# Keys of two batches by way of DRAM and a DMA transpose, with a new set-up and transfer model, in a fused block-sparse attention and MLP-mixer kernel

## The chip, the cores and the metric

The kernel runs on one core of one Trainium2 chip. The core has TensorE (PE, matmuls and transposes), VectorE (DVE), ScalarE (ACT), GpSimd (POOL) and SyncE (SP), which compute or issue work each in its own fixed order, and 16 DMA engines. SP, ACT and POOL issue transfers, each from a queue of its own. The metric is the device time of one execution in microseconds (us); lower is better.

## The reference

Four batches, eight heads, 768 positions, head dimension 64. Attention is limited, for each query, to the three blocks of 64 keys with the best gate score and to its own block, and is causal. Then comes one mixer layer: an MLP over positions and an MLP over channels.

```python
k_rep = k.reshape(B, H, n_blocks, block, D).mean(axis=3)
gate_scores = np.einsum('bhsd,bhnd->bhsn', q, k_rep)
gate_scores = np.where(causal, gate_scores, -1000000000.0)
top_idx = np.argsort(gate_scores, axis=-1)[..., -top_k:]
# mask: blocks in top_idx and the own block, and key position <= query position
scores = scale * np.matmul(q, k.transpose(0, 1, 3, 2))
scores = np.where(mask, scores, -1000000000.0)
attn = softmax(scores)
attn_out = np.matmul(attn, v)

x = attn_out.transpose(0, 2, 1, 3).reshape(B, S, H * D)
h = np.maximum(x.transpose(0, 2, 1) @ w_tok1, 0.0) @ w_tok2
u = x + h.transpose(0, 2, 1)
out = u + np.maximum(u @ w_ch1, 0.0) @ w_ch2
```

Inputs and output are fp32. The matmuls of the scores, of attention times V and of the MLPs run in fp16, the gate in fp32, since its order decides which blocks are taken.

## The kernel before, in words

**Pairs.** Two heads of one batch make a pair, numbered i = 0 to 15; pairs 0 to 3 are batch 0, 4 to 7 batch 1, and so on. For each pair:

- `load_qk` (L241) brings keys and queries in as [128, 6, 128] fp32 tiles `kl` and `ql`, in pieces of 256 bytes; `load_v` (L251) does so for the values. SP issues them.
- `transposes` (L330, matmuls on L336) turns each tile by six fp32 transposes on PE against an identity, into the PSUM tiles `tkl` and `tql`. `evac_t` (L339) copies them to SBUF on ACT as `kt` and `qt`; `cast` (L348) makes fp16 of them on POOL, once for each head, into the buffers KA (keys) and Q (queries).
- `ksum` (L354) sums the keys of each block on DVE, `kcopy` (L362) places the sums, `gate` (L372) multiplies queries by them on PE (five fp32 matmuls), and `gm`, `top`, `below`, `bias` (L381 to L413) make from it, on DVE, a bias of 0 or -30000 for each query and block.
- `mask` (L415) transposes the bias on PE, and `put_mask` (L425) writes it into twelve spare rows of Q. The same rows of KA hold an indicator of the block of each key, so that the score matmul adds the bias by itself. KA and Q have 128 rows for each head, 64 of data, twelve of these, and zeros.
- `scores` (L432) on PE, `expo` (L450) on ACT, the causal cut `diag` (L458) on DVE, `av` (L465) on PE, `recip` and `norm` (L477, L485) on DVE.

KA is one tile `KAX` with four slots (R = 4): the pair i uses slot i mod 4.

**MLP.** For each batch: `tok1`, `relu1`, `umix`, `uadd` make u (L497 to L559). u of batch 0 is transposed on PE (`utr`, L561); u of the other batches is stored to a DRAM scratch and loaded back by a transposing DMA (`store_u` L317, `turn_u` L324, issued by SP). Then `ch1` (L579) and `ch2` (L601) on PE with `relu2` and `oadd` on ACT and DVE, and `store` (L617) to the output. The ten weight loads are issued by POOL, which also casts them to fp16 on the way (L637 to L642).

**Who sets the order.** Nothing is decided while the kernel runs. `plan` (L66) is a list scheduler that runs at build time: every piece of work is an `Op` with an engine, an assumed duration, dependences, a priority and the ring buffers that it takes. It yields the order in which the work is emitted, and each engine runs its work in that order. Attention of pair i has priority 10 i and more, its preparation (`pre`) ten less, the MLP of a batch b 1000 (b + 1) and more: MLP work fills what attention leaves. `SP` in the plan are input loads, in the order of priority; `SPO` are stores and turns; both are the same engine. A transfer of assumed length `size` begins 1250 ns after its issue or when the one before has ended, and lands 700 ns after its end. `free` (L69) gives the time from which each engine can take work of the plan.

**The second key route** is in the code already and is taken by pairs i >= VIA; with VIA = 16, by none. In it `load_k8` (L267) loads the keys as [96, 2, 8, 64]: each of 96 rows of SBUF takes eight neighbouring positions, 2 KB in one piece; the tile takes one of the two `kt` buffers. `ksum8` (L277) sums over the eight on DVE, and `ksum_pe` (L284), one fp32 matmul with the constant `blk`, sums groups of eight rows, so that the block sums come without a transposed copy of the keys. `cast_k8` (L291) casts on POOL into the fp16 tile K16, which has 256 columns for each position: 64 keys of the first head, 64 with the block indicator, 64 with the indicator, 64 keys of the second head (`k16_zero` and `k16_ind`, L307 to L315, fill the padding once). `store_k` (L297) writes that to a DRAM scratch, and `turn_k` (L304) brings it back transposed:

```python
return lambda: nc.sync.dma_start_transpose(out=KAX[:, i % R, :, :], in_=T["kscr", i])
```

one transfer that writes the whole slot, keys, indicators and zeros of both heads. SP issues both; the store waits for the cast, the turn for the store and for the scores of pair i - 4.

**Set-up** (L828 to L864) runs before the planned work: constants by ACT's DMA queue, the zero rows of KA and of Q for slots 1 to 3 on POOL, other fills on DVE, and two transfers from ACT's queue that write the indicator rows of KA.

Of the kernel before, what the change touches and what calls it, by code (L numbers as in the profile page):

```python
# [9 lines left out]
FP = mybir.dt.float32  # L10
F16 = mybir.dt.float16
# [17 lines left out]
R = 4  # L29
FIRST = 4  # L30
TRI = 1
EARLY = 1
VIA = 16
UVIA = 1
LEAD = 960.0
WARM, COLD, WARM_END = 120, 20, 17000.0
IDLE = 1e9


class Op:  # L40
# [25 lines left out]
def plan(ops, rings, near=60.0):  # L66


    free = dict(PE=900.0, ACT=5500.0, DVE=4500.0, POOL=5000.0, SP=750.0, SPO=750.0)  # L69
    slots = {name: [(0.0, None)] * n for name, n in rings.items()}  # L70
    dma_free = 0.0
    waiting = {}
    users = {}
    ready = {e: [] for e in free}
    done = {}
    for op in ops:
        n = 0
        for d in op.deps:
            users.setdefault(id(d), []).append(op)
            n += 1  # L80
        waiting[id(op)] = n
        if n == 0:
            ready[op.eng].append(op)

    def finish(op, eng):
        return done[id(op)] + (LAT.get(eng, 33) if op.size == 0 else 60)

    def buf_free(buf, eng):
        t = 0.0
        for u in buf.users:  # L90
            if id(u) not in done:
                return None
            t = max(t, finish(u, eng))
        return t

    order = []
    left = len(ops)
    while left:
        best = None
        for o in [o for o in ready["PE"] if o.prio == IDLE and free["PE"] > WARM_END]:  # L100
            ready["PE"].remove(o)
            done[id(o)] = free["PE"]
            left -= 1
        if not left:
            break
        for e, cand in ready.items():
            if not cand:
                continue
            lst = []
            if e == "SP":  # L110
                if any(x.eng == e and x.prio < min(c.prio for c in cand) for x in ops if id(x) not in done):
                    continue
                cand = [min(cand, key=lambda c: c.prio)]
            for op in cand:
                t = free[e]
                for d in op.deps:
                    t = max(t, finish(d, e))
                ok = True
                for buf in op.takes:
                    first = None  # L120
                    for s, (_, old) in enumerate(slots[buf.ring]):
                        f = 0.0 if old is None else buf_free(old, e)
                        if f is not None and (first is None or f < first[0]):
                            first = (f, s)
                    if first is None:
                        ok = False
                        break
                    t = max(t, first[0])
                    buf.slot = first[1]
                if ok:  # L130
                    lst.append((t, op))
            if not lst:
                continue
            t0 = min(t for t, _ in lst)
            pick = min((x for x in lst if x[0] <= t0 + near), key=lambda x: (x[1].prio, x[0]))
            if best is None or pick[0] < best[0]:
                best = pick
        assert best is not None, "the plan cannot go on"
        t, op = best
        op.start = t  # L140
        for buf in op.takes:
            slots[buf.ring][buf.slot] = (0.0, buf)
        free[op.eng] = t + op.occ
        if op.size:
            begin = max(t + 1250, dma_free)
            dma_free = begin + op.size
            done[id(op)] = dma_free + 700
        else:
            done[id(op)] = t + op.rec
        ready[op.eng].remove(op)  # L150
        order.append(op)
        left -= 1
        for u in users.get(id(op), []):
            waiting[id(u)] -= 1
            if waiting[id(u)] == 0:
                ready[u.eng].append(u)
    return order, max(done.values())
# [3 lines left out]
def kernel(  # L161
# [11 lines left out]
    nc = tc.nc  # L173
# [52 lines left out]
    def op(eng, occ, rec, deps, prio, fn, takes=(), size=0):  # L226
        o = Op(eng, occ, rec, deps, prio, fn, takes, size)
        ops.append(o)
        return o
# [7 lines left out]
    def dve(occ, deps, prio, fn, takes=()):  # L237
        return op("DVE", occ, occ + 84, deps, prio, fn, takes)
# [71 lines left out]
    def k16_ind(y):  # L310
        def f():
            for c in (64, 128):
                nc.gpsimd.tensor_copy(out=K16[y][:, :, c:c + NB],
                                      in_=blk.rearrange("p (o n) -> p o n", o=1).broadcast_to([96, 8, NB]))
        return f  # L315

    def store_u(b):  # L317
# [107 lines left out]
    def put_mask(i, x):  # L425
        def f():
            lo = 64 if x == 0 else 0
            nc.vector.tensor_copy(out=QA[i % R][x][lo:lo + NB, 128:S], in_=T["bps", i][lo:lo + NB, :])  # L428
        return f
# [198 lines left out]
    O = {}  # L628
# [16 lines left out]
    for i in range(NP):  # L645
# [5 lines left out]
        def last_scores(x):  # L651
            return [O.get(("sc", old, x, g)) for g in range(3)]

        if i >= VIA:
            kb = Buf("kt")
            ld = op("SP", 500, 0, [], pre - 12, load_k8(i), [kb], size=1400)
            O["ksum", i] = dve(1100, [ld], pre + 1, ksum8(i))
            nb = Buf("bank")
            O["kpe", i] = pe(115, [O["ksum", i]], pre + 1, ksum_pe(i), [nb])
            O["kcopy", i] = dve(260, [O["kpe", i], O.get(("gate", old))], pre + 1, kcopy(i))  # L660
            nb.users.append(O["kcopy", i])
            y = i % 2
            if i < VIA + 2:
                O["kz", y] = op("POOL", 1100, 1150, [], pre - 1, k16_zero(y))
                O["ki", y] = op("POOL", 400, 450, [O["kz", y]], pre - 1, k16_ind(y))
            O["castk", i] = op("POOL", 1150, 1200, [ld, O["ki", y], O.get(("kst", i - 2))], pre + 3, cast_k8(i))
            kb.users += [O["ksum", i], O["castk", i]]
            O["kst", i] = op("SPO", 600, 0, [O["castk", i], O.get(("cast", "kt", i, 0))], pre + 3.1, store_k(i), size=1600)
            O["kturn", i] = op("SPO", 600, 0, [O["kst", i]] + last_scores(0) + last_scores(1), pre + 3.2, turn_k(i), size=2500)
            O["cast", "kt", i, 0] = O["cast", "kt", i, 1] = O["kturn", i]  # L670
        for t32, src, off in (("kl", k, 0), ("ql", q, 0.1))[i >= VIA:]:
            bf = Buf(t32)
            O[t32, i] = op("SP", 950, 0, [], pre - 12 + off, load_qk(i, t32, src), [bf], size=1900)
# [10 lines left out]
            big.users.append(O[name, i])  # L684
            dst = KA if name == "kt" else QA
            for x in range(2):
                O["cast", name, i, x] = op("POOL", 770, 825, [O[name, i]] + last_scores(x), pre + 4 + off,
                                           cast(dst, name, i, x))
                tb.users.append(O["cast", name, i, x])
            if name == "kt":  # L690
# [20 lines left out]
        mb = Buf("bank")  # L711
        O["mask", i] = pe(280, [O["bias", i]], pre + 4, mask(i), [mb])
        for x in range(2):
            O["put", i, x] = dve(410, [O["mask", i]] + last_scores(x), pre + 4, put_mask(i, x))
            mb.users.append(O["put", i, x])
        for x in range(2):
            for g in range(3):
# [23 lines left out]
            ab.users.append(O["norm", i, x])  # L741

    for n, (at, f) in enumerate(wq):
        after = O["cast", "kt", 3, 1] if n < 2 else O["cast", "qt", 3 + (n - 2) // 2, 1]
        W.append(op("POOL", 700, 0, [after], at, f, size=2900))

    for b in range(B):
        fill = 1000.0 * (b + 1)
# [79 lines left out]
    with tc.manual_schedule():  # L828
# [8 lines left out]
        own1 = np.where(nidx[None, None, :] == mrow, 0.0, MASKV).astype(np.float32)  # L837
        ind_np = (np.arange(S)[None, :] // 64 == nidx[:, None]).astype(np.float16)
        m0_np = (np.arange(128)[None, :] >= np.arange(128)[:, None]).astype(np.float16)
        gbias = const("gbias", np.concatenate([gb1, gb1], axis=2), FP, nc.scalar)  # L840
        own = const("own", np.concatenate([own1, own1], axis=2), FP, nc.scalar)
        ident16 = const("id16", np.eye(128, dtype=np.float16), F16, nc.scalar)
# [7 lines left out]
        nc.vector.memset(QA[0][1][0:64, :], 0.0)  # L850
        for r in range(R):
            nc.vector.memset(bn16[r], 0.0)
        for r in range(1, R):
            nc.gpsimd.memset(QA[r][0][64:128, :].bitcast(FP), 0.0)
            nc.gpsimd.memset(QA[r][1][0:64, :].bitcast(FP), 0.0)
        for r in range(R + 1):
            nc.vector.memset(V16[r][:, :, :, 64:65], 1.0)
        tri = const("tri", (MASKV * (1.0 - m0_np)).astype(np.float16), F16, nc.scalar)
        blk = const("blk", (np.arange(96)[:, None] // 8 == nidx[None, :]).astype(np.float32), FP, nc.scalar)
        m0 = const("m0", np.stack([m0_np, m0_np], axis=1), F16, nc.scalar)  # L860
        ind_dram = nc.inline_tensor(np.ascontiguousarray(np.broadcast_to(ind_np[:, None, :], (NB, R, S))), name="indc").ap()
        for x in range(2):
            lo = 64 * (1 - x)
            nc.scalar.dma_start(out=KAX[lo:lo + NB, :, x, :], in_=ind_dram)  # L864

        for o in order:
            o.fn()
# [33 lines left out]
```

## Time and profile before

| | |
|---|---|
| median of 5 runs | 276.88 us (276.13 to 277.18) |
| the profiled execution, its own time | 276.88 us |
| its span, first to last instruction | 275.1 us |
| granted TensorE clock, mean | 0.998 |
| instructions | 5930 |
| DMA | 34.67 MB, mean 126 GB/s |

The span leaves out 1.8 us of the time, before the first and after the last instruction. Busy time of an engine is the sum over its instructions; of a matmul the modelled end is a little after the start of the next, so the time that one group takes from PE is read from start to start. PEld is the weight load, which overlaps the matmul. A line of the profile names line, engine, operation and tiles as output<-input, with what an idle engine waited for in brackets. The DMA share is the mean over 16 engines; with packets of two queues at once it goes over 1.

### The profile page before, as it was taken

To read this page: it belongs to the slowest core of one execution; us is meant where nothing else is said; L and a number is where in the kernel's file an instruction comes from. 1 tells how busy PE (TensorE), PEld (TensorE's weight loads), DVE (VectorE), ACT (ScalarE), POOL (GpSimd) and SP (SyncE) were. 2 spreads that over 40 slices of the span, in tenths; PEclk is the share of its full clock that TensorE was granted. 3 is DMA by queue.
4 is the path that set the end of the run, shared out by engine and by line. 5 is a ranking of instruction groups with operands and counts; after the bars stand their busy time and mean duration, and the time that the engine had idled before them with its cause. 6 is when DMAs were issued, how large, how long until landed. Compare 5 with 4: busy or idle time off the path is not lost.

```text
span 275.1 us, 5930 instructions
## 1 busy us (share of the span) xinstructions
PE 263.1 (96%) x2309; PEld 174.3 (63%) x2309; DVE 163.5 (59%) x561; ACT 141.9 (52%) x188; POOL 79.1 (29%) x108
## 2 busy tenths in 40 slices
PE   7799989889999999999999999999999999999995
PEld 5678567779777878777777545654455544455543
DVE  5378968799988887886998433325323261243232
ACT  2356988578788888888886602440014410044100
POOL 8467903974543366435440000000000000000000
PEclk9999999999999999999999999999999999999999
DMA  8999999999798599760007222003740006720033
GB/s 168 197 220 203 182 207 224 214 225 218 158 226 167 117 182 200 166 146 2 1 22 194 94 75 80 0 0 116 178 167 2 0 0 209 174 77 0 4 114 114
DMA packets 94628, 34.67 MB, mean 126 GB/s; under 512 B 85672, under 2 KB 91144, under 8 KB 94600
## 3 DMA queue, kind: packets, MB, share of 16 engines
q1 hardware_dynamic: 90272, 29.89, 49.0%
q0 software_dynamic: 3232, 3.93, 8.4%
q10 hardware_dynamic: 1096, 0.47, 0.9%
q8 instruction: 18, 0.29, 0.5%
q14 instruction: 10, 0.08, 0.1%
HBM read 27.21 MB, written 8.65 MB: 130 GB/s over the span
## 4 chain that ended last, share of the span: by engine, by line
PE 72%; DVE 12%; issue 5%; POOL 4%; DMA 2%; ACT 1%; ACTq 1%; SPq 0%; DVEq 0%; POOLq 0%
PE c L606 22%; PE c L585 22%; PE sps L442 8%; PE gps L377 5%; PE aps L473 4%; PE tok L504 3%; PE ups L516 2%; DVE e L462 2%; PE tql L336 2%; DMA ql<-in_q_dram 2%; PE tkl L336 2%; DVE m L394 2%; DVE Q L428 1%; DVE u L524 1%; DVE kst L359 1%
## 5 line engine op out<-in xcount | busy, mean ns | idle before, releaser
L455 ACT ACTIVATE e<-sps 128x1024 f16<-128x1024 f32 (+1 forms) x96 | 84.1, 918 | 19.8 <-PE sps L442 14.3
L585 PE MATMUL c<-uT,wc 128*128 128x256 f16 (+1 forms) x384 | 67.8, 326 | 0.0
L595 ACT ACTIVATE h<-c 128x512 f16<-128x512 f32 x48 | 28.7, 598 | 72.7 <-PE c L585 72.1
L606 PE MATMUL c<-wc,h 128*128 128x512 f16 (+2 forms) x300 | 64.0, 370 | 0.0
L585 PEld LDWEIGHTS <-wc 128*128 128x128 f16 x384 | 37.3, 98 | 23.9
L442 PE MATMUL sps<-Q,KA 128*128 128x512 f16 (+3 forms) x256 | 50.0, 305 | 2.5 <-ACT e L455 1.0
L606 PEld LDWEIGHTS <-h 128*128 128x128 f16 x300 | 28.8, 98 | 32.0 <-issue 0.6
L597 DVE TENSOR_SCALAR h<-c 128x256 f16<-128x256 f32 x48 | 20.2, 420 | 34.9 <-PE c L585 34.9
L614 DVE TENSOR_TENSOR ob<-u,c 128x512 f32<-128x512 f16 (+2 forms) x25 | 16.6, 665 | 39.5 <-PE c L606 39.5
L351 POOL CAST KA<-kt 64x768 f16<-64x768 f32 x32 | 26.8, 838 | 45.3 <-ACT kt L345 44.2
L462 DVE TENSOR_TENSOR e<-e,m 128x256 f16<-128x256 f16 x90 | 32.3, 363 | 12.3 <-ACT e L455 11.3
L442 PEld LDWEIGHTS <-KA 128*128 128x128 f16 x256 | 22.7, 101 | 16.7 <-issue 3.9
L351 POOL CAST Q<-qt 64x768 f16<-64x768 f32 x32 | 26.9, 842 | 4.6 <-ACT qt L345 3.1
L473 PE MATMUL aps<-V,e 128*128 128x65 f16 x672 | 27.1, 193 | 1.2 <-DVE e L462 1.0
L473 PEld LDWEIGHTS <-e 128*128 128x128 f16 x672 | 25.6, 98 | 3.8 <-DVE e L462 1.3
L377 PE MATMUL gps<-ks,qt 128*128 128x24 f32 x160 | 20.3, 269 | 1.9 <-ACT qt L345 1.4
L377 PEld LDWEIGHTS gps<-ks,qt 128*128 128x128 f32 x160 | 19.1, 191 | 4.5 <-ACT qt L345 1.6
L345 ACT COPY kt<-tkl 128x768 f32<-128x768 f32 x16 | 12.8, 799 | 14.1 <-DMA m<-m0c 7.1
L492 DVE TENSOR_TENSOR x<-aps,rc 128x384 f16<-128x384 f32 x32 | 17.7, 552 | 0.6
L263 POOL CAST V<-v 128x768 f16<-128x768 f32 x16 | 13.3, 836 | 15.1 <-DMA v<-in_v_dram 14.4
L428 DVE COPY Q<-bps 12x640 f16<-12x640 f16 x32 | 15.5, 484 | 1.1
L359 DVE TENSOR_REDUCE kst<-kt 128x12 f32<-128x768 f32 x15 | 14.1, 941 | 1.4 <-ACT kt L345 1.4
(52 smaller groups left out, 214.2 us busy)
## 6 DMA issues: line engine op xcount, KB each, us to landing
kl<-in_k_dram SPq DMA_DIRECT2D x32, 192.0 KB, 4.4
ql<-in_q_dram SPq DMA_DIRECT2D x32, 192.0 KB, 4.3
v<-in_v_dram SPq DMA_DIRECT2D x16, 384.0 KB, 5.3
out_dram<-ob SPq DMA_DIRECT2D x23, 256.0 KB, 2.1
wc<-in_moe_w_ch_dram POOLq DMA_DIRECT2D x8, 384.0 KB, 8.8
uscr<-u SPq DMA_DIRECT2D x3, 768.0 KB, 3.7
w<-in_moe_w_tok_dram POOLq DMA_DIRECT2D x2, 384.0 KB, 7.7
out_dram<-ob SPq DMA_DIRECT2D x1, 160.0 KB, 1.8
```

Of the source, the lines that this page charges most:

```text
L351: nc.gpsimd.tensor_copy(out=dst[i % R][x][lo:lo + 64, :], in_=T[name, i][lo:lo + 64, :])
L377: nc.tensor.matmul(out=g[:, j, :], lhsT=T["qt", i][:, 128 * j + 128:128 * j + 256], rhs=ks2[i % R], start=True, stop=True)
L428: nc.vector.tensor_copy(out=QA[i % R][x][lo:lo + NB, 128:S], in_=T["bps", i][lo:lo + NB, :])
L442: nc.tensor.matmul(out=p[:, off + a:off + a + n], lhsT=KA[i % R][x][:, 128 * kk:128 * kk + 128], rhs=QA[i % R][x][:, q0 + a:q0 + a + n], s ...
L455: nc.scalar.activation(out=e[:, 0:width], in_=T["sps", i, x, g][:, 0:width], func=AF.Exp, scale=scale)
L462: nc.vector.tensor_tensor(out=d, in0=d, in1=m0, op=ALU.mult)
L473: nc.tensor.matmul(out=p[:, jq, :], lhsT=T["e", i, x, g][:, o:o + 128], rhs=V16[i % (R + 1)][:, x, kk, :], start=(kk == 0), stop=(kk == jq))
L492: nc.vector.tensor_tensor(out=T["x16", b][:, :, 64 * hh:64 * hh + 64], in0=T["aps", i, x][:, :, 0:64], in1=T["rc", i, x].broadcast_to([128 ...
L585: nc.tensor.matmul(out=p, lhsT=wc1_16[:, cc, 128 * fc:128 * fc + 128], rhs=T["uT", b][:, cc, a:e], start=(cc == 0), stop=(cc == NCC - 1))
L595: nc.scalar.activation(out=T["h2", b][:, fc, a:e], in_=T["c1", b, fc, n], func=AF.Relu)
L597: nc.vector.tensor_scalar(out=T["h2", b][:, fc, a:e], in0=T["c1", b, fc, n], scalar1=0.0, scalar2=None, op0=ALU.max)
L606: nc.tensor.matmul(out=T["c2", b, j, lo], lhsT=T["h2", b][:, fc, 128 * j:128 * j + 128], rhs=wc2_16[:, fc, lo:hi], start=(fc == 0), stop=( ...
```

## The change

- `VIA` goes from 16 to 8: pairs 8 to 15 (batches 2 and 3) take the second key route.
- The plan's model of transfers: SP and SPO share the issue time; transfers issued by POOL have a lane of their own and slow the others that are in flight by 0.8 of their size; weight loads have sizes of 3200 and 2100 instead of 2900; ACT is free from 4800 instead of 5500 and POOL from 7500 instead of 5000.
- Set-up: the indicator rows of KA, `blk` and `m0` are loaded from POOL's queue instead of ACT's. The zero rows of Q for slots 1 to 3 are no longer filled in the set-up but by three planned operations, `zero_q`, on POOL, for which the casts and masks of pairs 1 to 3 wait.
- `WAIT` writes out the casts after which each weight load is issued; they are the ones that the expression before gave.

```diff
-VIA = 16
+VIA = 8
+WAIT = [("kt", 3, 1), ("kt", 3, 1), ("qt", 3, 1), ("qt", 3, 1), ("qt", 4, 1), ("qt", 4, 1),
+        ("qt", 5, 1), ("qt", 5, 1), ("qt", 6, 1), ("qt", 6, 1)]
...
-    free = dict(PE=900.0, ACT=5500.0, DVE=4500.0, POOL=5000.0, SP=750.0, SPO=750.0)
+    free = dict(PE=900.0, ACT=4800.0, DVE=4500.0, POOL=7500.0, SP=750.0, SPO=750.0)
     slots = {name: [(0.0, None)] * n for name, n in rings.items()}
-    dma_free = 0.0
+    dma_free = swd_free = 0.0
+    flying = {}
...
         free[op.eng] = t + op.occ
-        if op.size:
+        if op.eng in ("SP", "SPO"):
+            free["SP"] = free["SPO"] = t + op.occ
+        if op.size and op.eng == "POOL":
+            begin = max(t + 1500, swd_free)
+            swd_free = begin + op.size
+            done[id(op)] = swd_free + 1200
+            for o, (a, e) in list(flying.items()):
+                if e > begin:
+                    flying[o] = (max(a, begin), e + 0.8 * op.size)
+                    done[id(o)] += 0.8 * op.size
+            dma_free = max([dma_free, begin + 0.8 * op.size] + [e for _, e in flying.values()])
+        elif op.size:
             begin = max(t + 1250, dma_free)
             dma_free = begin + op.size
             done[id(op)] = dma_free + 700
+            flying[op] = (begin, dma_free)
+            for o in [o for o, (_, e) in flying.items() if e < t]:
+                del flying[o]
...
+    def zero_q(r):
+        def f():
+            nc.gpsimd.memset(QA[r][0][64:128, :].bitcast(FP), 0.0)
+            nc.gpsimd.memset(QA[r][1][0:64, :].bitcast(FP), 0.0)
+        return f
...
+        zq = [op("POOL", 880, 930, [], pre - 1, zero_q(i))] if 0 < i < R else []
...
-                O["cast", name, i, x] = op("POOL", 770, 825, [O[name, i]] + last_scores(x), pre + 4 + off,
+                O["cast", name, i, x] = op("POOL", 770, 825, [O[name, i]] + zq + last_scores(x), pre + 4 + off,
                                            cast(dst, name, i, x))
...
-            O["put", i, x] = dve(410, [O["mask", i]] + last_scores(x), pre + 4, put_mask(i, x))
+            O["put", i, x] = dve(410, [O["mask", i]] + zq + last_scores(x), pre + 4, put_mask(i, x))
...
-        after = O["cast", "kt", 3, 1] if n < 2 else O["cast", "qt", 3 + (n - 2) // 2, 1]
-        W.append(op("POOL", 700, 0, [after], at, f, size=2900))
+        W.append(op("POOL", 700, 0, [O[("cast",) + WAIT[n]]], at, f, size=3200 if n < 2 else 2100))
...
+        ind_dram = nc.inline_tensor(np.ascontiguousarray(np.broadcast_to(ind_np[:, None, :], (NB, R, S))), name="indc").ap()
...
-        for r in range(1, R):
-            nc.gpsimd.memset(QA[r][0][64:128, :].bitcast(FP), 0.0)
-            nc.gpsimd.memset(QA[r][1][0:64, :].bitcast(FP), 0.0)
...
-        blk = const("blk", (np.arange(96)[:, None] // 8 == nidx[None, :]).astype(np.float32), FP, nc.scalar)
-        m0 = const("m0", np.stack([m0_np, m0_np], axis=1), F16, nc.scalar)
-        ind_dram = nc.inline_tensor(np.ascontiguousarray(np.broadcast_to(ind_np[:, None, :], (NB, R, S))), name="indc").ap()
         for x in range(2):
             lo = 64 * (1 - x)
-            nc.scalar.dma_start(out=KAX[lo:lo + NB, :, x, :], in_=ind_dram)
+            nc.gpsimd.dma_start(out=KAX[lo:lo + NB, :, x, :], in_=ind_dram)
+        blk = const("blk", (np.arange(96)[:, None] // 8 == nidx[None, :]).astype(np.float32), FP, nc.gpsimd)
+        m0 = const("m0", np.stack([m0_np, m0_np], axis=1), F16, nc.gpsimd)
```

## The prediction

> **What bounds the kernel now.** I read the engine totals and slices of the page first, then the table of busy time by stage, then the timelines of the places that the change touches.
>
> ```profile
> span 275.1 us, 5930 instructions
> ...
> PE 263.1 (96%) x2309; PEld 174.3 (63%) x2309; DVE 163.5 (59%) x561; ACT 141.9 (52%) x188; POOL 79.1 (29%) x108
> ...
> DMA  8999999999798599760007222003740006720033
> ```
>
> TensorE is busy 96% of the span, no other engine over 59%. The DMA row says where the second limit lies: the 16 DMA engines are at 70% or more in nearly all of the first 18 slices (to 124 us), then mostly idle.
>
> ```profile
> 40.00:60.00 20.00, 18.03 (x242) 15.30 (x238) 16.62 (x62) 15.22 (x22) 12.29 (x16) 1.00 1.13 222
> 60.00:80.00 20.00, 18.90 (x249) 15.38 (x249) 18.67 (x69) 15.14 (x20) 10.15 (x13) 1.00 1.07 199
> 80.00:100.00 20.00, 19.99 (x218) 15.48 (x217) 16.17 (x64) 17.63 (x24) 9.74 (x12) 1.00 0.75 149
> 100.00:120.00 20.00, 20.00 (x237) 15.63 (x236) 16.41 (x75) 17.62 (x24) 10.11 (x13) 1.00 0.99 197
> 120.00:140.00 20.00, 20.00 (x215) 14.82 (x214) 17.63 (x66) 16.48 (x22) 8.27 (x10) 1.00 0.09 19
> ```
>
> After the time come PE, weight load, DVE, ACT and POOL busy, the granted clock, the DMA share and GB/s. From 80 us PE has no gap, at full clock, and that holds until about 272 us, because work of the MLP stage fills what attention leaves. So after 80 us **the end is a sum of PE work**: a microsecond of matmul removed there is a microsecond off the end, if no new gap opens. Before 80 us PE idles 8.8 us by the same table (1.97 of it from 40 to 60, 1.10 from 60 to 80).
>
> **Part 1: eight key transposes leave PE.** Pairs 8 to 15 are loaded, transposed and scored from about 50 to 150 us, mostly in the stretch without gaps.
>
> ```profile
> 66.67 0.82 PE L336 MATMUL tkl<-id,kl 128*128 128x128 f32 x6
> 67.33 0.82 PE L336 MATMUL tql<-id,ql 128*128 128x128 f32 x6
> 67.98 0.50 PE L566 MATMUL utps<-id,u 128*128 128x128 f16 x6
> ```
>
> From start to start (ends overlap) six fp32 transposes take 67.33 - 66.67 = 0.66 and 67.98 - 67.33 = 0.65 us. Eight key tiles: 8 x 0.655 = **-5.24 us**. In their place each pair gets one fp32 matmul for the block sums. No such row exists; the nearest is the gate, five fp32 matmuls shown as ten records in 1.08 us, 0.22 us each. Bounds: half of that, one record, 0.11 (8 x = 0.9), and twice, for one that stands alone between fp16 work, 0.44 (3.5). I take 0.22: **+1.76 us**.
>
> Off PE the edit costs nothing by itself. ACT loses eight copies of 0.80 us. POOL swaps two casts of 0.84 for one over 1024 columns, by their rate 0.84 x 1024/768 = 1.12. DVE's block sum stays near 0.94 and two tiny copies read PSUM: some 0.25 us more a pair on an engine that is busy 68.9 of 80 us from 60 to 140. The cover for that is MLP work on PE; without it, it would cost 8 x 0.25 = 2.0 us, inside part 4's bounds. The two zero fills and indicator copies (about 3 us of POOL) fall where POOL is half idle.
>
> **Part 2: set-up.**
>
> ```profile
> 4.28 0.33 ACTq L197 DMA_DIRECT2D tri<-tric  x1
> 5.31 0.33 ACTq L197 DMA_DIRECT2D blk<-blkc  x1
> 6.63 0.34 ACTq L197 DMA_DIRECT2D m<-m0c  x1
> 7.08 2.27 ACTq L864 DMA_DIRECT2D KA<-indc  x2
> 9.39 0.80 ACT L345 COPY kt<-tkl 128x768 f32<-128x768 f32 x1 [7.14 <-DMA m<-m0c]
> 10.08 0.80 ACT L345 COPY qt<-tql 128x768 f32<-128x768 f32 x1
> ```
>
> ACT's first key copy stands behind four loads that its own queue still has to issue (5.31 to 9.35), although PE ended the transposes at 6.2. The change moves these to POOL. Then ACT is free at 4.61, copies keys from 6.3 to 7.1, and the queries, whose transposes ended at 8.4, from about 8.3 to 9.1, instead of 10.88: the gate starts 1.8 us earlier. Is POOL late then? Its eight fills of KA end at 3.76; four issues at the 0.53 to 0.98 us that weight loads take there end at 5.9 to 7.7; four casts of 0.84 follow, to 11.2 at the latest. The first score comes 5.4 us after the gate (10.94 to 16.31 before), so near 14.5: covered. The indicator loads start some 3 us earlier than before and land in time. The six fills of Q, now three planned operations (6 x 0.41 = 2.5 us), go into POOL's idle time (2.10 us before 20.32) and the 2.5 us that their old place frees.
>
> How much of 1.8 survives? The early loads come at the pace of a full DMA: V of pair 2, issued at 21.28 with 5.3 us to landing, is cast at 26.99, with 0.4 us to spare. An earlier chain meets it. Bounds -1.8 and 0; I take **-1.0 us**.
>
> The Trainium skill bears on this in "DMA: Bandwidth & Descriptors", Rules for kernel authors: spreading DMAs over several engines brings no bandwidth, only the issue time of the sequencer. The row above has exactly such issue time on the path, 9.35 - 4.61 = 4.7 us of ACT's queue; by the rule the bytes moved buy nothing more, and a gain through faster landing would be 0.
>
> **Part 3: the corrected model.** It costs no instruction; it changes the order in which each engine gets its work, which is fixed at build time.
>
> ```profile
> 33.33 1.13 POOL L640 DMA_DIRECT2D wc<-in_moe_w_ch_dram  x2
> 45.98 0.83 POOL L263 CAST V<-v 128x768 f16<-128x768 f32 x1 [11.52 <-DMA v<-in_v_dram]
> 46.75 2.11 POOL L351 CAST KA<-kt 64x768 f16<-64x768 f32 x2
> ```
>
> Weight loads delay V of pair 4, and POOL stands 11.5 us in front of it with the key and query casts of the next pair behind. A plan that knows this puts those casts first. PE had other work meanwhile, so at most the gaps from 40 to 60 us come back: -1.97 to 0. I take **-0.5 us**, as other gaps there wait for DVE and ACT.
>
> **Part 4: what the DMA route costs.** Per pair it removes a 393 KB load in 256-byte pieces, adds one in 2 KB pieces, a store of 393 KB to DRAM, and a transposing load of it. The only like rows are the store and turn of u, twice the size:
>
> ```profile
> uscr<-u SPq DMA_DIRECT2D x3, 768.0 KB, 3.7
> ...
> uT<-uscr SPq DMA_TRANSPOSE x3, 7.1
> ```
>
> At the 197 GB/s of the small-piece stretch the old load takes 2.0 us of all engines. At the 346 GB/s that u's store reaches, new load and store take 1.15 us each. The turn of u shows 127 to 152 GB/s in the windows of one or two microseconds where little else runs; half of u at the upper rate takes 2.6 us. Net 1.15 + 1.15 + 2.6 - 2.0 = 2.9 us a pair, 23.2 for eight. From 60 to 140 us the DMA was busy 21.4 + 15.0 + 19.8 + 1.8 = 58.0 us; with 23.2 it needs 81.2 of 80. The spare time that hid all transfers is gone. But attention may run late: MLP work of two batches is ready to fill PE, and the last batch is mixed only at 217 us.
>
> The Trainium skill gives 261 GB/s for such a turn ("DMA: Bandwidth & Descriptors", Latency and other measured facts), and 350 to 400 where the source is contiguous. By it the turn would be 1.5 us, and the DMA would need some 9 us less; the rows above show the slower rate, and I keep them.
>
> SP issues in order. Each store waits for POOL's cast, each turn for the store's landing (3.7 us for u), and behind both stand the next pair's key and query loads and a V load; who waits for these is PE's query transposes and POOL's casts, in order too. A turn also holds SP: 3.67 us for u, so about 1.84 here, while the kernel's plan reckons 0.6. So 1.24 us a pair can be late against the written order: 8 x 1.24 = 9.9 us at worst, if each lands as a gap on PE. At best nothing, or even the 1.1 us of gaps from 60 to 80 comes back. As the plan also reckons 9.1 us of transfer a pair (the rows above make it 2.0 + 2.0 + 1.15 + 1.15 + 2.6 = 8.9), it has its own slack and keys are due one pair ahead (9 us), I take the low end: **+0.5 us**.
>
> **Sum:** -5.24 + 1.76 - 1.0 - 0.5 + 0.5 = -4.5, so a span of 270.6 us. The profiled execution took 276.88, 1.8 around its span, and that is also the median of the runs. Predicted: **272.4 us**. With all favourable bounds, -5.24 + 0.9 - 1.8 - 2.0 - 1.1 = -9.2 (267.7); with no gain from order or start and 2 us of gaps, -1.5 (275.4): its own range.
>
> **Rivals.**
> *The SP queue becomes the bound (slower).* Place: store and turn in SP's order, pairs 8 to 15. Price 9.9 instead of 0.5: -4.5 + 9.4 = +4.9, **281.8 us**. It decides from (4.5 + 0.5)/8 = 0.6 us of gap a pair. For it: 81.2 of 80 us of DMA, and an order that can't adapt. Against: the pile of MLP work. 0.27.
> *Everything frees up.* The start keeps 1.8, POOL's wait gives back 2.0, no gaps: -5.24 + 1.76 - 3.8 = -7.3, **269.6 us**. For it: the chain of waits runs through both places. Against: the just-in-time V load. 0.15.
> *Hidden anyway.* PE loses its work but waits as long for keys or for DVE: four to five microseconds of gaps, **276.9 us**. Against: fill. 0.08, half of it within 0.2%.
> Forecast: 0.50.
>
> About 0.2% is what runs of this kernel can tell from no change. Faster 0.50 + 0.15 + 0.03 = 0.68; same 0.04; slower 0.27 + 0.01 = 0.28. The range must reach into the slower case: 267.5 to 281.0 leaves out its upper half (0.12) and little below.
>
> **What would show it.** Right: 48 fewer transposes, PE without gaps from 80 us on, the first gate near 9.2 us, POOL's wait for V under 5 us, the end 4 to 5 us earlier. Wrong: PE gaps between 75 and 145 us released by a turn or a late V; SP standing several microseconds before a store; the start shifted but its gain gone by 40 us; block-sum matmuls far from 0.22 us.

## The result and the profile after

| | before | after |
|---|---|---|
| median of all runs | 276.63 us (50 runs, 275.87 to 279.46) | 279.56 us (29 runs, 277.06 to 283.12) |
| median without the slowest runs | 276.63 us (50 runs) | 279.0 us (21 runs) |
| ratio, after to before | | 1.0082 [1.0067, 1.0096] |
| the profiled execution, its span | 276.88, 275.1 | 279.45, 277.6 |
| DMA moved | 34.67 MB | 40.96 MB |

Runs more than 1.5% above the fastest of their kernel are left out of every ratio and of every median below, while the recorded expectations quote medians of all runs, up to 1 us higher. The change makes the kernel 0.8% slower. The forecast was 272.4 us and faster, so it had the wrong sign.

These are lines of the page after: its head, engine totals, the chain by engine (the work that ended last, followed back from the end, as shares of the span), and the group of the new block sum (busy time, mean ns of one, idle time before it).

```profile
span 277.6 us, 5848 instructions
PE 260.9 (94%) x2277; PEld 170.3 (61%) x2277; DVE 167.3 (60%) x561; ACT 135.7 (49%) x180; POOL 79.3 (29%) x110
PE 61%; DVE 17%; DMA 15%; SPq 2%; POOL 2%; issue 1%; ACT 1%; DVEq 0%; ACTq 0%; POOLq 0%
L298 DVE TENSOR_REDUCE kp<-k 96x128 f32<-96x1024 f32 x8 | 15.4, 1922 | 0.9 <-DMA k<-in_k_dram 0.9
```

The chain and the old block sum in the kernel before:

```profile
PE 72%; DVE 12%; issue 5%; POOL 4%; DMA 2%; ACT 1%; ACTq 1%; SPq 0%; DVEq 0%; POOLq 0%
L359 DVE TENSOR_REDUCE kst<-kt 128x12 f32<-128x768 f32 x15 | 14.1, 941 | 1.4 <-ACT kt L345 1.4
```

PE does 2.2 us less work (263.1 before) and the span is 2.5 us longer: the work left, and idle time came. In the chain PE fell from 72% to 61%, DVE rose from 12% to 17%, and DMA from 2% to 15%. The row to remember is the sum's: one block sum of the new layout takes 1.92 us, where the one it replaces takes 0.94.

The table of busy time by stage (after the time: PE, weight load, DVE, ACT, POOL, clock, DMA share, GB/s):

```profile
60.00:80.00 20.00, 19.06 (x208) 14.06 (x206) 17.15 (x62) 15.43 (x21) 10.16 (x12) 1.00 1.18 209
80.00:100.00 20.00, 17.13 (x185) 13.59 (x186) 19.30 (x75) 9.95 (x13) 12.54 (x15) 1.00 1.16 240
100.00:120.00 20.00, 19.06 (x196) 13.22 (x195) 16.06 (x60) 14.76 (x20) 5.50 (x7) 1.00 1.25 235
120.00:140.00 20.00, 18.71 (x205) 13.21 (x201) 18.26 (x65) 12.69 (x16) 7.46 (x10) 1.00 0.89 183
```

From 80 to 140 us PE was busy 20 of 20 before. Now it idles 2.87, 0.94 and 1.29 us, and in the worst stretch DVE is busy 19.30 of 20. What PE waited for between 80 and 142 us (engine, tile and line, releaser: us in total, times, longest):

```profile
PE kps L305 <- DVE kp L298: 2.3, 3, 1.1
PE bps L443 <- DVE bn L432: 1.5, 2, 1.1
PE kps L305 <- DVE u L547: 0.6, 1, 0.6
PE aps L496 <- DVE e L485: 0.4, 2, 0.3
```

Every line ends on DVE; none names a turned key tile or a transfer. Transfers stand one step behind: the block sums themselves waited 0.9 us in all for their keys (the 0.60 in the first row below is the longest). Two places of the timeline (start, duration, then the wait in brackets):

```profile
78.91 1.92 DVE L298 TENSOR_REDUCE kp<-k 96x128 f32<-96x1024 f32 x1 [0.60 <-DMA k<-in_k_dram]
...
80.88 0.39 PE L305 MATMUL kps<-blk,kp 96*128 96x12 f32 x2 [1.13 <-DVE kp L298]
...
97.66 0.45 PE L443 MATMUL bps<-id,bn 128*128 128x128 f16 x5 [1.09 <-DVE bn L432]
```

The sum ends at 80.83, and the matmul that reads it starts at 80.88: PE stood 1.13 us for it, with MLP work behind it in its queue that it may not overtake (it starts at 81.12). The last line is the same lateness one step on: the selection row `bn` stands on DVE at the end of a stretch of work without a pause, which begins with a sum at 92.72.

The larger DMA share of the chain has one place from 60 us on (start, duration):

```profile
64.44 12.19 DMA v<-in_v_dram
76.75 0.84 POOL V L280
77.59 1.67 SPq L318
79.36 5.66 DMA k<-in_k_dram
85.05 1.94 DVE kp L298
```

A V load lands late, a key store on SP waits for POOL, and the next key load stands behind that store; from 85 us on the chain is mostly DVE. Whether the sum or these transfers make the loss is what E4 and E13 ask.

### The profile page after: what moved, and what is told of

It is laid out like the page before. It is cut to its first block, busy times and chain, and to the rows that moved or that the text cites. A ratio compares the mean times of both kernels' runs of the same rounds, so it can differ in the third digit from the quotient of the medians.

```text
span 277.6 us, 5848 instructions
## 1 busy us (share of the span) xinstructions
PE 260.9 (94%) x2277; PEld 170.3 (61%) x2277; DVE 167.3 (60%) x561; ACT 135.7 (49%) x180; POOL 79.3 (29%) x110
## 2 busy tenths in 40 slices
DMA packets 96971, 40.96 MB, mean 148 GB/s; under 512 B 85872, under 2 KB 91144, under 8 KB 96944
## 4 chain that ended last, share of the span: by engine, by line
PE 61%; DVE 17%; DMA 15%; SPq 2%; POOL 2%; issue 1%; ACT 1%; DVEq 0%; ACTq 0%; POOLq 0%
PE c L629 22%; PE c L608 18%; DMA v<-in_v_dram 6%; PE sps L465 6%; DVE kp L298 4%; PE aps L496 4%; DMA ql<-in_q_dram 4%; PE tok L527 3%; DMA w<-in_moe_w_tok_dram 2%; DVE m L417 2%; PE ups L539 2%; DMA k<-in_k_dram 2%; DVE Q L451 2%; DVE e L485 2%; PE gps L400 2%; DVE x L515 1%
## 5 line engine op out<-in xcount | busy, mean ns | idle before, releaser
L629 PE MATMUL c<-wc,h 128*128 128x512 f16 (+2 forms) x300 | 65.3, 370 | 0.0
L465 PE MATMUL sps<-Q,KA 128*128 128x512 f16 (+3 forms) x256 | 48.7, 305 | 1.9 <-ACT e L478 1.0
L485 DVE TENSOR_TENSOR e<-e,m 128x256 f16<-128x256 f16 x90 | 27.6, 317 | 13.0 <-ACT e L478 12.8
L496 PE MATMUL aps<-V,e 128*128 128x65 f16 x672 | 27.8, 194 | 1.1 <-DVE e L485 0.7
L368 ACT COPY qt<-tql 128x768 f32<-128x768 f32 x16 | 12.8, 800 | 9.9 <-PE tql L359 9.9
L374 POOL CAST KA<-kt 64x768 f16<-64x768 f32 x16 | 13.3, 832 | 13.9 <-ACT kt L368 13.3
L280 POOL CAST V<-v 128x768 f16<-128x768 f32 x16 | 14.0, 876 | 9.0 <-DMA v<-in_v_dram 6.3
L298 DVE TENSOR_REDUCE kp<-k 96x128 f32<-96x1024 f32 x8 | 15.4, 1922 | 0.9 <-DMA k<-in_k_dram 0.9
```

Source lines behind the costliest of these rows:

```text
L298: nc.vector.tensor_reduce(out=t, in_=T["k8", i].rearrange("p g t d -> p g d t"), axis=AX.X, op=ALU.add)
L374: nc.gpsimd.tensor_copy(out=dst[i % R][x][lo:lo + 64, :], in_=T[name, i][lo:lo + 64, :])
L465: nc.tensor.matmul(out=p[:, off + a:off + a + n], lhsT=KA[i % R][x][:, 128 * kk:128 * kk + 128], rhs=QA[i % R][x][:, q0 + a:q0 + a + n], s ...
L485: nc.vector.tensor_tensor(out=d, in0=d, in1=m0, op=ALU.mult)
L496: nc.tensor.matmul(out=p[:, jq, :], lhsT=T["e", i, x, g][:, o:o + 128], rhs=V16[i % (R + 1)][:, x, kk, :], start=(kk == 0), stop=(kk == jq))
L629: nc.tensor.matmul(out=T["c2", b, j, lo], lhsT=T["h2", b][:, fc, 128 * j:128 * j + 128], rhs=wc2_16[:, fc, lo:hi], start=(fc == 0), stop=( ...
```

## The experiments

Span = PE's busy time + its idle time, and the idle time falls into three parts. The numbers come from the stage tables of the profiled executions (0 to 80, 80 to 142 us and the rest); the kernels in it are described below.

| us | before | E8: new model only | E1: all but the key route | E7: E1, old sum twice | E4: all, block sum cut | after |
|---|---|---|---|---|---|---|
| PE busy | 263.1 | 263.2 | 261.9 | 264.3 | 258.8 | 260.9 |
| PE idle before 80 | 8.6 | 4.5 | 6.7 | 4.2 | 8.2 | 8.1 |
| PE idle 80 to 142 | 0.0 | 0.1 | 0.1 | 2.8 | 1.1 | 5.1 |
| PE idle after 142 | 3.4 | 3.5 | 3.8 | 4.9 | 3.5 | 3.5 |
| span | 275.1 | 271.3 | 272.5 | 276.1 | 271.6 | 277.6 |

**Which part loses.** E1 takes the changed kernel and leaves all keys on PE.

```diff
-VIA = 8
+VIA = 16
```

> The changed kernel with no pair on the second key route: only the new set-up and the new transfer model are left. Theory (the loss lies in the block sums over the second layout, 1.92 us of DVE a pair): within 1 us of before, the five microseconds of PE gaps between 80 and 142 us are gone, 276 to 277 us. Rival (the new set-up and order lose time by themselves): 278 us or more.

Median 274.05 us, ratio 0.9901 [0.9871, 0.9931]. The gaps from 80 us are gone (0.1). So the slowdown is the key route's, 279.0 - 274.05 = 4.9 us, and the rest of the change gains 2.6.

E2 puts the route alone into the kernel before (there `VIA` from 16 to 8).

> The kernel before with pairs 8 to 15 on the second route, its set-up and its transfer model left as they were. Theory: the block sums cost DVE 1.9 us a pair here too, PE gaps of about 5 us behind them, 278 to 281 us. Rival (the new model's order makes the loss, the route itself gains): 274 us or less.

Median 287.17, ratio 1.0359 [1.0310, 1.0409]: +10.5 us, more than the 4.9 that it costs under the new model. Here the granted clock is lower too (mean 0.970; last section), so the old and the new price of the route don't add simply.

E8 has the changed `plan()` and transfer sizes alone: old set-up, old start times of ACT and POOL, no route.

```diff
+        if op.eng in ("SP", "SPO"):
+            free["SP"] = free["SPO"] = t + op.occ
+        if op.size and op.eng == "POOL":
...
-        W.append(op("POOL", 700, 0, [after], at, f, size=2900))
+        W.append(op("POOL", 700, 0, [after], at, f, size=3200 if n < 2 else 2100))
```

> The kernel before with the new transfer model alone: set-up, start times of the engines and key route as before. Tells what the 2.6 us that set-up and model gained together came from. If from the order alone: 274 to 275 us; if from the set-up: 276 to 277 us; half each: 275.3 us.

Median 273.66, ratio 0.9905 [0.9875, 0.9935]: faster than both kernels. The corrected order alone is worth 2.9 us; in the profiled executions all of the gain is idle time before 80 us (8.6 to 4.5 in the table). The new set-up adds nothing to it: E1 with it is at 274.05.

**The block sum on DVE.** E4 puts a copy of one key of eight in place of the sum, so it leaves seven of eight keys out of the gate's sums. The written order and all transfers, casts and matmuls of the route stay, and the copy takes 0.21 us (median).

```diff
-            nc.vector.tensor_reduce(out=t, in_=T["k8", i].rearrange("p g t d -> p g d t"), axis=AX.X, op=ALU.add)
+            nc.vector.tensor_copy(out=t, in_=T["k8", i][:, :, 0, :])
```

> The changed kernel with the block sum over the eight positions of a row replaced by a copy of the first of them (about 0.2 us of DVE instead of 1.92 a pair, same dependences, same written order); so seven of eight keys are left out of the gate's block sums of pairs 8 to 15. Theory DVE: PE gaps between 80 and 142 us fall from 5.1 to under 1.5 us, 274 to 276 us. Rival DMA and SP queue (keys or loads land too late): gaps stay at 4 us or more, 278 us or more.

Median 273.39, ratio 0.9888 [0.9833, 0.9942]. 5.6 us come back with one DVE instruction a pair, though the route's DMA work is all there. The stage table of E4:

```profile
80.00:142.00 62.00, 60.87 (x657) 44.64 (x655) 52.28 (x218) 41.70 (x54) 25.61 (x30) 1.00 1.16 235
```

DVE is busy 52.3 of 62 us, as in the kernel before (52.2; 55.2 after), and PE 60.9, at a DMA share of 1.16. The V and key loads of 64 to 85 us are gone from its chain, though it makes the same ones.

E7 goes the other way: no route, but the old block sum of pairs 8 to 15 is issued twice, 0.94 us more of DVE a pair.

```diff
-VIA = 8
+VIA = 16
...
-            nc.vector.tensor_reduce(out=kst, in_=kt.rearrange("p (n w) -> p n w", w=64), axis=AX.X, op=ALU.add)
+            for _ in range(2 if i >= 8 else 1):
+                nc.vector.tensor_reduce(out=kst, in_=kt.rearrange("p (n w) -> p n w", w=64), axis=AX.X, op=ALU.add)
```

> The changed kernel with no pair on the second route, but the block sum of pairs 8 to 15 issued twice on DVE (0.94 us more a pair; the plan isn't told). It measures the load on DVE by itself, without the DMA route. Theory DVE load: 8 x 0.94 = 7.5 us more of DVE turn into 2 to 5 us of PE gaps, 276 to 279 us. Rival (DVE has room, the harm needs the DMA route): under 275 us, no gaps from 80 to 140 us.

Median 278.56, ratio 1.0085 [1.0065, 1.0105], 4.5 us over E1 for 8 x 0.94 = 7.5 us of DVE work. PE's waits of E7 from 80 to 142 us:

```profile
PE gps L401 <- DVE ks L391: 2.8, 4, 0.8
```

The load alone, without a byte of the route's DMA, opens gaps of the same kind: the gate waits for a sum that is 0.7 us late, four times. These gaps are 2.8 of the 3.6 us by which its span exceeds E1's; the rest of the table's differences (PE's busy time is 2.4 us longer for the same matmuls, idle time before 80 us 2.5 shorter) isn't explained. E4 and E7 together show the effect of the load from both sides.

E6 turns half the pairs (`VIA` 12).

> The changed kernel with only batch 3 (pairs 12 to 15) on the second route. Theory DVE load, each pair adds its share: half way between no pair (274.05) and eight (279.56), 276 to 277.5 us. Rival (the harm comes only where the stretch from 60 to 100 us, with weight loads, u of batch 0 and the first pairs of the route, is full): near or below no pair, 272 to 274.5 us, since four pairs still save about 1.75 us of PE.

Median 278.04, ratio 1.0042 [1.0012, 1.0072]: 4.0 us over E1, more than half of 4.9. The cost isn't so much a pair; PE idles 4.2 us from 80 to 142.

**DMA and SP's queue.** E13 stores each turned pair's tile twice, the second time to a place that nothing reads: one more 393 KB transfer and one more issue on SP a pair.

```diff
+            t2 = dram.tile([S, 256], F16, tag=f"kd{i % 2}", name=f"kdup_{i}")
+            nc.sync.dma_start(out=t2.rearrange("(p t) c -> p (t c)", t=8), in_=K16[i % 2].rearrange("p t c -> p (t c)"))
```

> The changed kernel with the store of the padded keys issued twice, the second to a scratch that nobody reads: 393 KB more of DMA and one more issue on SP for each of eight pairs, by the earlier rows 1.15 us of all DMA engines and 0.4 us of SP a pair. Theory DVE: within 1 us of the changed kernel, 278.5 to 280.5 us. Rival (DMA and SP queue are the bound from 60 to 140 us): 8 x 0.5 to 1.2 us more, 283 us or more.

Median 279.68, ratio 1.0120 [1.0065, 1.0176]. 0.7 us over the changed kernel, and the changed kernel's interval lies inside this one. If the DMA set the end, an estimated 8 x 1.15 = 9 us would have shown. So in this kernel the DMA share of 1.1 to 1.25 is not the bound, as far as a store can show it; no run makes the turns longer.

**Can the written order or another engine carry the sum?** The plan reckons 1.1 us for it. E5 tells it 1.9 (`dve(1100, ...)` to `dve(1900, ...)` for `ksum8`).

> The changed kernel with the one assumed duration of the block sum in the plan corrected from 1100 to 1900 ns; the same instructions in another order. Theory order (the gaps come from PE work written too early behind a sum that ends later than planned): gaps fall to 2 us or less, 275 to 276.5 us. Theory DVE load (DVE is full, whatever the order): gaps stay above 3.5 us, 278 us or more.

Median 279.15, ratio 1.0073 [1.0019, 1.0126]: no change. E17 stretches all DVE durations in the plan by 1.1, as the profile shows DVE fuller than planned.

```diff
-        return op("DVE", occ, occ + 84, deps, prio, fn, takes)
+        return op("DVE", 1.1 * occ, 1.1 * occ + 84, deps, prio, fn, takes)
...
-            O["ksum", i] = dve(1100, [ld], pre + 1, ksum8(i))
+            O["ksum", i] = dve(1750, [ld], pre + 1, ksum8(i))
```

> The changed kernel, same instructions, with every assumed DVE duration of the plan raised by 10% and the block sum at 1.1 x 1750 = 1925 ns: the written order leaves DVE the time that its rows show, those stretched behind POOL included. Theory (the gaps are PE work written ahead of a DVE result that the plan believes to be earlier): gaps from 80 to 140 us under 2.5 us, 275 to 277.5 us. Rival (DVE is simply full there): 279 us or more.

Median 276.63, ratio 1.0021 [0.9988, 1.0055]. The stage table of E17:

```profile
80.00:142.00 62.00, 59.70 (x634) 44.03 (x631) 59.54 (x216) 43.94 (x55) 28.80 (x34) 1.00 1.08 225
```

The gaps fall from 5.1 to 2.3 us: about half was PE work written down ahead of DVE results that the plan believed done, and E5 shows that correcting the sum alone doesn't reach it. Now DVE itself is busy 59.5 of 62 us, close to full. E18 is the control, the same stretch on E8, without the route.

> The kernel before with the new transfer model alone and the same 10% on the DVE durations. Under the theory a small gain or none on 273.7 us, since from 80 us on that kernel shows no gaps: 272.5 to 274 us. Rival (any new order moves the time by 1% either way): outside of that.

Median 273.69, ratio 0.9888 [0.9858, 0.9917]: level with E8. Slack in the plan helped only where DVE was late.

E3 writes the sum as four additions of contiguous rows on DVE.

```diff
-            nc.vector.tensor_reduce(out=t, in_=T["k8", i].rearrange("p g t d -> p g d t"), axis=AX.X, op=ALU.add)
+            nc.vector.tensor_tensor(out=h, in0=k8[:, :, 0:2, :], in1=k8[:, :, 2:4, :], op=ALU.add)
+            nc.vector.tensor_tensor(out=h, in0=h, in1=k8[:, :, 4:6, :], op=ALU.add)
+            nc.vector.tensor_tensor(out=h, in0=h, in1=k8[:, :, 6:8, :], op=ALU.add)
+            nc.vector.tensor_tensor(out=t, in0=h[:, :, 0, :], in1=h[:, :, 1, :], op=ALU.add)
```

> The changed kernel with the block sum over the second layout made of four contiguous additions (3 x 256 and 128 elements a row) instead of one strided reduction; estimated from the rows of DVE at 1.2 to 1.4 us instead of 1.92, some 0.6 us less a pair. Theory DVE: between the changed kernel (279.6) and the one without the sum (274.4), by 0.6 of 1.7 us saved: 276 to 278 us, PE gaps from 80 to 140 us under 4 us. Rival (it was the dropped sum's effect on something else, and the strided read itself doesn't matter): 279 us or more.

Median 282.81, ratio 1.0232 [1.0185, 1.0279], a miss: the four means add up to 0.52 + 0.66 + 0.55 + 0.42 = 2.15 us, not less than 1.92 (last section). E9 puts the same four on POOL (`nc.gpsimd`, planned at 2600 ns).

> The changed kernel with the block sum of pairs 8 to 15 on POOL (four additions, planned at 2600 ns) instead of DVE. Theory DVE: DVE loses 1.92 us a pair and the gaps behind it, 274 to 276.5 us. Rival (a busier POOL stops DVE's two-input operations, as the row of the tree version suggests, so the load comes back on DVE as longer rows): DVE's mean rows grow, 278 us or more.

Median 278.29, ratio 1.0068 [1.0039, 1.0098]. They take 0.73 + 0.75 + 0.77 + 0.52 = 2.77 us there. Moving the sum alone doesn't cure it. In the execution that was profiled (281.35 us, 3 us above this median) the rows fit the rival that was named: DVE's `bn` takes 0.59 us on average, 0.35 in the changed kernel, and PE's longest waits from 80 us on stand before `bps`, behind it:

```profile
98.86 1.18 DVE L437 SCALAR_TENSOR_TENSOR bn<-lt,own 128x120 f16<-128x120 f32 x1
...
100.10 0.45 PE L448 MATMUL bps<-id,bn 128*128 128x128 f16 x5 [1.34 <-DVE bn L437]
```

E12 below, with its sums on POOL too, has `bn` at 0.38 us, so how much of this the usual run of E9 shows is not known.

**The idle time before 80 us.** After 20 us, one line of PE's timeline and one of POOL's in the changed kernel:

```profile
24.75 1.85 POOL L325 MEMSET K<- 96x1024 f32 x2
...
37.00 0.84 PE L558 MATMUL tok<-x,w 128*128 128x128 f16 x12 [1.22 <-DMA w<-in_moe_w_tok_dram]
```

The zero fills of the new scratch tile stand on POOL ahead of the weight loads, and PE waits for a weight. E11 lets the fills wait for a later cast.

```diff
-                O["kz", y] = op("POOL", 1100, 1150, [], pre - 1, k16_zero(y))
+                O["kz", y] = op("POOL", 1100, 1150, [O["cast", "qt", 5, 1]], pre - 1, k16_zero(y))
```

> The changed kernel with the two zero fills of the padded tile K16 (1.85 us of POOL at 24.8 us, ahead of the weight loads) made to wait for the query casts of pair 5. Theory (they push the first weight load from 29.0 to 30.0 us and PE's first MLP matmul waits for it): the wait of 1.2 to 2.2 us near 36 us falls under 1 us, and the time falls by about 1 us, to 278 to 279 us. Rival (that gap is made good later): 279.5 us or more.

Median 280.20, ratio 1.0132 [1.0075, 1.0188]: a miss. The wait for the weight halves to 0.6 us, and one of 2.7 appears where `kps` stands behind DVE's `h`. Behind that stands a transfer:

```profile
76.11 1.89 DVE L298 TENSOR_REDUCE kp<-k 96x128 f32<-96x1024 f32 x1 [2.30 <-DMA k<-in_k_dram]
...
78.39 0.39 PE L305 MATMUL kps<-blk,kp 96*128 96x12 f32 x2 [2.73 <-DVE h L620]
```

DVE had nothing to do for 2.3 us until the keys of that pair landed, 9.6 us after SP issued the load at 66.50. So here the rival that was set aside in the changed kernel, transfers that land too late, opens the longest gap. E14 does the same on E4.

> The changed kernel with the block sum replaced by a copy of one of eight positions (seven of eight keys left out of the gate's sums of pairs 8 to 15) and the zero fills late. Without the sum the route saved 3.1 us of PE work and gained nothing on the kernel with no pair on it (274.4 against 274.05). Theory (the fills ahead of the weight loads ate 1.5 us of it, the rest is gaps of a DVE queue that is still full): 272 to 273.5 us. Rival (the fills don't matter, each new order brings gaps of its own): 274.5 us or more.

Median 275.00, ratio 0.9938 [0.9915, 0.9961]; the new gap comes here as well (2.0 us), so it isn't the sum's: DVE's copy waits 3.2 us for the same load. E12 joins E11 to E9, the sums on POOL.

> Both edits: block sum on POOL and the zero fills late. If both theories hold, this keeps the 3.5 us of PE work that the route saves and beats both kernels: 271.5 to 274 us, below the 273.7 us of the model alone at best. If POOL's load stops DVE: 277 us or more.

Median 274.73, ratio 0.9922 [0.9892, 0.9952]: the only full route that beats the kernel before, though not E8. DVE has 43.1 us of work from 80 to 142. Its one long wait of PE, 2.06 us, ends a chain of POOL work that starts with a V load landing at 73.1 us (last section). E15 is E12 with half the pairs (`VIA` 12).

> Block sum on POOL, zero fills late, and only batch 3 on the route, whose loads come when the weight loads are over. PE saves 4 x 0.45 = 1.8 us against no pair on it. Theory (the route pays where the sum finds an engine with room): 271.5 to 273.5 us, the best so far. Rival (each written order brings its own gaps): 275 us or more.

Median 275.88, ratio 0.9978 [0.9949, 1.0008], on the rival's side. E16 splits the sums, even pairs on POOL, odd ones on DVE.

> Zero fills late, all eight pairs on the route, their block sums in turn on POOL (even pairs) and on DVE with its true 1900 ns in the plan (odd pairs). Theory DVE: half of DVE's added load is gone, between 275.2 (all on POOL, fills late) and 280.2 (all on DVE, fills late): 276.5 to 279 us. Rival (a balance of the two beats both): under 275 us.

Median 281.55, ratio 1.0204 [1.0168, 1.0240], slower than either whole and outside what both theories gave. PE waits 2.31 us up to 78.53, again behind a sum that DVE starts 2.30 us late for its keys, and the granted clock then falls to 0.50 (last section). Each edit writes a new order of the whole program with gaps of its own, and between such neighbours a few microseconds couldn't be foreseen here from the load of one engine.

## Why the prediction was wrong

**The step that failed** is in part 1: "Off PE the edit costs nothing by itself", with "DVE's block sum stays near 0.94". It took the price of a sum over 768 contiguous elements a partition in groups of 64, 941 ns (1.22 ns each), for one over 1024 elements in groups of eight that lie 256 bytes apart, which takes 1922 ns (1.88 each); the count of elements alone would have made it 1255. So each pair puts 1.0 us on DVE instead of 0.25, on an engine that I had read as busy 68.9 of 80 us. The cover that I named, MLP work on PE, stands in PE's queue behind the matmul that waits for the sum. E4 takes the sum out and gains 5.6 us; E7 adds such a load without the route and loses 4.5.

**Part 4's term** therefore has the wrong place and size: +0.5 for gaps behind the DMA, 5.1 measured behind DVE. Its rival, SP's queue at 281.8, had the direction right, but not the cause: a turn holds SP 1.4 to 5.1 us (median 2.9; I took 1.84), the DMA share is over 1, yet no wait of PE ends on a turn, E4 keeps all these transfers, and E13 doubles the store for 0.7 us. It isn't nothing either: late loads stand in the chain from 64 to 85 us and open the longest gap of E11, E14 and E16. "Hidden anyway" named DVE and "four to five microseconds of gaps" and got 0.08; that was the mechanism, on top of which the kernel lost more.

**Term by term**, on the spans of the two profiled executions:

- PE's work: -5.24 + 1.76 = -3.5 predicted; E1 to E4, 261.9 to 258.8, shows -3.1. Right, and the block-sum matmul takes 0.14 to 0.24 us from start to start in the changed kernel, as the 0.22 assumed. Only 2.2 is seen from before to after. Why PE's busy time is 2.1 longer there than in E4 stays open.
- Set-up, -1.0: wrong. The first gate came at 10.57 (10.94 before, 9.2 foreseen). The profile has the cause: queries landed later and their transposes started at 8.69 instead of 7.54, after a wait of 1.15 us for the load. E1, with the same set-up, had its gate at 9.90, and beside E8 it shows no gain that lasts.
- Order, -0.5: the mechanism was right and the size wrong. POOL's wait for V fell from 11.5 to 2.1 us at most, as foreseen, and E8 alone is worth 2.9 us. I had capped it at the gaps from 40 to 60 us; E8 closes those (1.97 to 0.24 us of idle time) and shortens others before and after them. The 8.8 us of idle time that the prediction reads before 80 us are 8.6; its sum doesn't use them. In the changed kernel the gain isn't seen: idle before 80 us is 8.1 instead of E8's 4.5. Part 1's "two zero fills ... fall where POOL is half idle" is 1.2 us of this (the wait for the weight); the remainder was not pinned down.
- Sum on the spans: -2.2 of work, -0.5 before 80 us, +5.1 of gaps, +0.1 after 142: +2.5, against -4.5.

Of the signs named beforehand, 48 fewer transposes and the shorter V wait came true; PE without gaps and the gate at 9.2 didn't.

**What stays open:** why the route gains next to nothing even without the sum. E4 (273.39) and E14 (275.00) have about 3 us less PE work than E1 (274.05), and their intervals overlap with E1's. Their idle time before 80 us is 1.4 and 1.0 us longer than E1's: E4 waits 2.2 us for a weight (E1 0.8), E14 has in its place the 2.0 us behind the late keys. Then 1.1 and 2.3 us of gaps follow, all but a little behind DVE, and these have no shown cause. E11 and E14 show that mending the wait for the weight brings another, for a load on SP's queue.

**The version to keep** is E8, the corrected model alone, at 273.66 us; E18 is level with it.

## What to carry to other kernels

Price a moved reduction by a row of its own form (layout and length of the groups), not by its element count, and look first at how full its new engine is in that stage. When one engine's queue order is fixed, work behind a late instruction is no cover for it. When a wait names an engine, look at what that engine waited for: E11's gap names DVE, and DVE was idle for a load. A more truthful cost model may be worth more than the transfers that it was made for: test it by itself.

## What the hardware showed

**A strided sum on DVE.** Sums of eight elements that lie 256 bytes apart cost 1.88 ns an element, against 1.22 for sums of 64 contiguous ones, and that row hardly varies (1.92 or 1.93 us on average in every run that kept it). No run separates the stride from the shorter groups, of which there are 128 a partition instead of 12.

**DVE and POOL on two inputs.** In E3's timeline the four additions take:

```profile
77.30 1.94 POOL L316 CAST K<-k 96x1024 f16<-96x1024 f32 x1 [0.77 <-DMA k<-in_k_dram]
...
77.93 0.41 DVE L300 TENSOR_TENSOR kh<-k 96x256 f32<-96x256 f32 x1
...
78.38 1.14 DVE L301 TENSOR_TENSOR kh<-kh,k 96x256 f32<-96x256 f32 x1
...
79.55 0.42 DVE L302 TENSOR_TENSOR kh<-kh,k 96x256 f32<-96x256 f32 x1
```

Two equal additions take 0.42 and 1.14 us; the long one ran while POOL's cast did, which took 1.94 where five of the eight take 1.03 (the addition at 77.93 ran beside it too, unstretched). The reduce of one input, 1.90 to 1.94 us in the changed kernel, was never stretched, not even at 78.91 beside a cast. The Trainium skill ("SBUF — State Buffer", SBUF: two separate sides) says that a DVE operation with two SBUF inputs and a reading GpSimd operation lock each other out; these rows agree, and E3 is the price: unstretched, the four would take 0.41 + 0.42 + 0.42 + 0.29 = 1.54 us instead of 2.15.

**PE's clock after a short gap.** E12's stage table, two microseconds a line, where PE had waited 2.06 us up to 82.94:

```profile
80.00:82.00 2.00, 0.88 (x5) 0.29 (x3) 1.96 (x13) 0.00 (x0) 1.88 (x3) 1.00 1.35 219
82.00:84.00 2.00, 1.06 (x9) 0.87 (x9) 0.19 (x1) 1.73 (x3) 1.94 (x4) 0.95 1.47 135
84.00:86.00 2.00, 2.00 (x14) 2.00 (x12) 1.80 (x4) 0.60 (x1) 1.88 (x3) 0.50 1.00 217
...
90.00:92.00 2.00, 2.00 (x15) 1.06 (x13) 1.69 (x4) 1.15 (x2) 1.84 (x4) 0.84 0.99 266
```

The granted clock goes to 0.50 for six microseconds (the lines between show 0.50 too): at half speed six microseconds do the work of three, so by this estimate the gap of 2 us cost some 3 us more. E2's table shows the same from 102 to 112 us, after a stretch with PE busy 0.92 of 2, and E16's from 82 to 86, after its wait of 2.31 us. It doesn't always come. In E11 PE waited 2.73 us up to 78.39:

```profile
76.00:78.00 2.00, 0.00 (x0) 0.00 (x0) 1.89 (x2) 0.00 (x0) 1.04 (x1) 1.00 1.10 144
78.00:80.00 2.00, 1.61 (x11) 1.18 (x12) 1.83 (x6) 1.11 (x2) 1.00 (x2) 1.00 0.92 308
```

The clock stayed at 1.00, in this table to 84 us. The Trainium skill ("TensorE: Matmul & The Clock Gate", Part 1: The HAM clock gate) puts the slow clock after an idle window of about 3.4 us; here a wait of 2.06 us was followed by it and one of 2.73 us was not. The measurement decides: the length of a single wait doesn't tell the two apart.
